# Loading the q weights of a decode kernel in two column halves, one issued by SyncE and one by ScalarE

## The chip, the cores and the metric

The kernel runs on one core of a Trainium2 chip. The metric is the device time of one execution, in microseconds (us); lower is better. Where two kernels are compared, both ran on the same chip in alternating rounds. Single executions of the same kernel fall on two close levels about 1 us apart (for the kernel before on one chip, 379.8 to 380.3 and 380.9 to 381.3), so a difference of half a microsecond between medians means little here.

## The reference

One decode step for 4 sequences: attention over the last 4096 positions of a cache, then a gated MLP, both with a residual.

```python
x: (4, 1, 576)   k_cache, v_cache: (4, 16, 16384, 128)   wq: (576, 4096)   wo: (4096, 576)
q = layernorm(x) @ wq                      # 32 query heads of 128
k, v = the last 4096 positions of the caches, each of the 16 heads used by 2 query heads
o = softmax(q k^T / sqrt(128)) v
h = x + o @ wo
gate, up = layernorm(h) @ W_gate, layernorm(h) @ W_up      # (576, 4608) each
h2 = h + (relu(gate) * up) @ W_down                        # (4608, 576)
```

All is bf16. With 4 tokens every weight and every cache entry is used for hardly any arithmetic: about 160 MB must be read from HBM for a few small products.

## The kernel before

A helper class `Prog` collects the instructions of each engine in program order and turns named dependencies into semaphore waits. `P.dma("sync", ...)` issues a load from SyncE, `P.dma("scalar", ...)` from ScalarE. Each engine works through its own list in order.

The loads go into an arena in SBUF with a ring of four 4 MB slots. Here is their order; all but the load of x are issued by SyncE (names shortened, cuts marked):

```python
NSLOT = 4; TILE = 16384; QWW = 8192        # columns of bf16 per partition

def place(name, off, size, reader, make, key=None):
    # waits for the last reader of every 64-column block it overwrites, then:
    P.dma("sync", ("L",) + name, make, semk, deps)

s = ring_slot()                            # wq: rows 0..511 as [128 partitions, 4 rows x 4096]
wq_off = slot0 + s * TILE
place(("wq", 0), wq_off, TILE, "QMM",
      lambda e: e.dma_start(out=arena[:, wq_off:wq_off + TILE], in_=main_rows(A_wq)), key=f"slot{s}")
P.dma("sync", ("L", "wq", 1), ...)         # the last 64 rows of wq, 0.5 MB
for g in range(NTILE):                     # 16 tiles of K and of V, 4.2 MB each
    add_kv("K", g)
    if g >= 4:
        add_kv("V", g - 4)
# ... the last V tiles, wo, W_gate, W_up, W_down
```

So the ring is filled in the order wq, K0, K1, K2, then K3 in the slot of wq, K4 in that of K0, V0 in that of K1, K5 in that of K2, V1 in that of K3, K6 in that of K4, and so on. A load into a used slot is issued only when the last reader is done: K3 after the q matmuls (`QMM`), K4 after the scores of tile 0.

The path from x to the first scores:

```python
act("warm_sqrt", ...)                                   # ScalarE's list before the change starts here
P.dma("scalar", ("L", "x"), lambda e: e.dma_start(out=x_bf, in_=A_x ...), "d_x")     # 4.5 KB
# VectorE: layer norm of x (bn_stats ... xn); PE: transposes; VectorE: xnT
for c in range(5):                                      # contraction chunks of 128 (the last of 64)
    for bk in range(2):
        for g in range(4):
            # chunk c < 4 reads columns c*4096.. of the wq slot, chunk 4 the 0.5 MB piece
            deps = {0: [("L", "wq", 0), "xnT", "c_xnT"], 4: [("L", "wq", 1)]}.get(c, [])   # at bk == g == 0
            pe(...)
# ScalarE and VectorE: q out of PSUM; PE: regroup; ScalarE: 8 copies of q into the score layout ("QW")
# VectorE: transpose each K tile in place (two halves, "TRA"); PE: scores, after "TRA" and for tile 0 after "QW"
```

VectorE transposes all 16 K tiles, and between the two halves of tile 4 it also does the softmax work of the first sequence.

Of the kernel before, what the change touches and what calls it, by code (L numbers as in the profile page):

```python
# [25 lines left out]
TILE = 16384  # L26
QWW = 8192
# [5 lines left out]
def mm_same(e, out, lhsT, rhs, start, stop, tile, pos):  # L33
    return e.add_instruction(mybir.InstMatmult(  # L34
        name=e.bass.get_next_instruction_name(), engine=mybir.EngineType.PE, ins=[e.lower_ap(rhs), e.lower_ap(lhsT)],
        outs=[e.lower_ap(out)], start_tensor_calc=start, stop_tensor_calc=stop, tile_size=tile, tile_position=pos,
        ldweights=False, bass_skip_group_check=True))
# [85 lines left out]
def bass_sequential_preLN__sliding_block_cached__glu_gated_reglu__decode_kernel(  # L123
# [12 lines left out]
    with ExitStack() as es:  # L136
        cnt = [0]

        def sb(name, shape, dt):
            return es.enter_context(nc.sbuf_tensor("sb_" + name, shape, dt))  # L140

        P = Prog()
# [8 lines left out]
        arena = sb("arena", [128, AW], BF16)  # L151
# [26 lines left out]
        xnT = sb("xnT", [128, DC + 1, 32], BF16)  # L178
# [36 lines left out]
        owner = {}  # L215
# [3 lines left out]
        def place(name, off, size, reader, make, key=None):  # L219
            deps = []  # L220
            for blk in range(off // 64, (off + size) // 64):
                r = owner.get(blk)
                if r is not None and r not in deps:
                    deps.append(r)
                owner[blk] = reader
            semk = key or "d_" + "_".join(str(v) for v in name)
            P.dma("sync", ("L",) + name, make, semk, deps)
            land[name] = off
# [3 lines left out]
        def ring_slot():  # L232
            s = ring[0] % NSLOT
            ring[0] += 1
            return s
# [12 lines left out]
        def main_rows(W):  # L248
            return W[0:512, :].rearrange("(p r) n -> p (r n)", r=4)

        def last_rows(W):
            return W[512:576, :].rearrange("r (a n) -> (r a) n", a=2)

        s = ring_slot()
        wq_off = slot0 + s * TILE
        place(("wq", 0), wq_off, TILE, "QMM",
              lambda e: e.dma_start(out=arena[:, wq_off:wq_off + TILE], in_=main_rows(A_wq)), key=f"slot{s}")
        P.dma("sync", ("L", "wq", 1), lambda e: e.dma_start(out=pT[:, 0:2048], in_=last_rows(A_wq)), "d_wq1")
        for g in range(NTILE):
            add_kv("K", g)  # L260
# [22 lines left out]
        for j in range(4):  # L283
            wd_off.append(off)
            for r0, r1 in ((0, 9),) if j < 3 else ((0, 6), (6, 8), (8, 9)):
                place(("wd", j, r0), off + r0 * D, (r1 - r0) * D, ("DOWN", 1),
                      lambda e, off=off, j=j, r0=r0, r1=r1: e.dma_start(  # L287
                          out=arena[:, off + r0 * D:off + r1 * D],
                          in_=B_W_down[j * 1152:(j + 1) * 1152, :].rearrange("(p r) n -> p (r n)", p=128)[:, r0 * D:r1 * D]))
# [18 lines left out]
                                                in_=c_qm[:, :, :].rearrange("p q (h j) -> p q h j", j=4),  # L308
# [4 lines left out]
                                                in_=to_v[:, :, :].rearrange("p n (k a) -> p n k a", a=4),  # L313
# [60 lines left out]
        def pe_q():  # L374
            for c in range(DC):
                for bk in range(2):
                    for g in range(4):
                        n = 4 * bk + g
                        w = arena[:, wq_off + c * H * DH + n * 512:][:, 0:512] if c < 4 else pT[:, g * 512:g * 512 + 512]
                        deps = []  # L380
                        if bk == g == 0:
                            deps = {0: [("L", "wq", 0), "xnT", "c_xnT"], 4: [("L", "wq", 1)]}.get(c, [])
                        if c < 4 and bk:
                            fn = lambda e, c=c, w=w, g=g, bk=bk: mm_same(e, bank[4 + bk][32 * g:32 * g + 32, :], xnT[:, c, :], w,
                                                                         c == 0, False, (128, 32), (0, 32 * g))
                        else:
                            fn = lambda e, c=c, w=w, g=g, bk=bk: e.matmul(  # L387
                                bank[4 + bk][32 * g:32 * g + 32, :], lhsT=xnT[:, c + bk if c == 4 else c, :], rhs=w,
                                start=(c == 0), stop=(c == 4), skip_group_check=True)
                        pe("QMM" if bk else "QMM0", fn, deps)  # L390
            for blk in range(8):
                pe("QT", lambda e, blk=blk: e.matmul(
                    bass.AP(tensor=psb, offset=7 * 512 + blk // 4 * 16 + blk % 4, ap=[[4096, 128], [4, 4], [32, 4]]),
                    lhsT=bass.AP(tensor=pp, offset=4096 + blk * 128, ap=[[PPW, 128], [1, 128]]),
                    rhs=bass.AP(tensor=ident_b, offset=0, ap=[[128, 128], [32, 4], [1, 4]]),
                    start=True, stop=True, skip_group_check=True), [f"qev{blk // 4}"] if blk % 4 == 0 else [])
# [166 lines left out]
        pe_x()  # L563
        dve_x()
        pe_q()
        act_q()
        dve_q()
# [49 lines left out]
        for a in range(8):  # L617
            for n in range(2):
                for j in range(4):
# [4 lines left out]
                    else:  # L624
# [6 lines left out]
                                             in_=bass.AP(tensor=psb, offset=512 + 224, ap=[[4096, 128], [1, 64], [0, 2]])), ["part1"])  # L631
# [28 lines left out]
        for g in range(2):  # L660
            for c in (4, 0, 1, 2, 3):
                part_ = c if c == 4 or (c == 3 and g) else 0
                for m in range(3):
                    for j in range(4):
                        first = m == 0 and j == 0 and (c in (0, 4) or part_ == 3)
                        deps = [("L", "gu", g, part_)] if first else []
# [36 lines left out]
        for j in range(4):  # L703
            wv = arena[:, wd_off[j]:wd_off[j] + WDJ].rearrange("p (r n) -> p r n", n=D)
            for r in range(9):
                for n in range(2):
                    deps = []
# [11 lines left out]
        for n in range(2):  # L719
            P.dma(("sync", "scalar")[n], ("O", n), lambda e, n=n: e.dma_start(  # L720
                out=orow[:, 288 * n:288 * n + 288], in_=bass.AP(tensor=out_sb, offset=32 * n * 288, ap=[[8 * 288, 4], [1, 288]])),
# [31 lines left out]
```

## Time and profile before

| | before |
|---|---|
| median time | 380.82 us (3 runs, 380.12 to 381.21; a fourth was taken with the change, below) |
| span of the profiled run | 378.4 us (that run took 380.22 us) |
| moved | 159.76 MB, mean 422 GB/s |
| PE, VectorE busy | 56%, 61% of the span |

These are the lines of the page of before that show what limits it. The row of digits gives the mean busy share of the 16 DMA engines in 40 slices of the span, in tenths (9 is 90% or more); the row below it gives what they moved.

```profile
span 378.4 us, 2668 instructions
...
DMA  8999999999999999999999999999999999999994
GB/s 333 443 441 429 414 433 440 443 426 416 435 434 443 423 421 436 436 440 419 423 436 436 436 423 429 435 436 433 423 429 438 429 436 423 441 421 422 416 426 190
...
q1 hardware_dynamic: 6632, 159.59, 98.4%
...
DMA 61%; PE 19%; DVE 15%; issue 4%; SPq 1%
```

The DMA engines are busy for 90% or more of every slice between the first and the last. No compute engine comes near that. The chain of waits that ended last (the final line) is mostly DMA. In the first slice only 333 GB/s were moved: 3.15 MB in 9.46 us, which at 436 GB/s (what many of the full slices moved) is 7.2 us of work, so by this estimate the start costs about 2.2 us.

The next lines are from the timeline of before: start, duration, engine, line, operation and, in brackets, the idle time before it and what ended it. SPq and ACTq are the issues of loads by SyncE and ScalarE.

```profile
0.73 0.38 SPq L257 DMA_DIRECT2D sb_arena<-in_A_wq_dram  x1
...
0.90 0.56 ACTq L343 DMA_DIRECT2D sb_x_bf<-in_A_x_dram  x1
...
5.67 0.81 DVE L345 BATCH_NORM_STATS2 sb_bn<-sb_x_bf 4x6 f32<-4x288 bf16 x2 [2.68 <-DMA sb_x_bf<-in_A_x_dram]
...
12.98 0.62 PE L387 MATMUL psb<-sb_arena,sb_xnT 128*32 128x512 bf16 x4 [4.23 <-DMA sb_arena<-in_A_wq_dram]
...
16.37 0.98 PE L387 MATMUL psb<-sb_pp,sb_xnT 128*32 128x512 bf16 x8
...
20.80 9.69 ACT L422 COPY sb_arena<-sb_q_keep 32x256 bf16<-32x256 bf16 x8
...
23.96 8.77 DVE L431 STREAM_TRANSPOSE sb_arena<-sb_arena 128x4096 f32<-128x4096 f32 x2 [2.38 <-DMA sb_arena<-in_A_k_cache_dram]
...
32.79 0.66 PE L455 MATMUL psb<-sb_arena 128*32 128x512 bf16 x4 [12.63 <-DVE sb_arena L431]
...
34.09 8.77 DVE L431 STREAM_TRANSPOSE sb_arena<-sb_arena 128x4096 f32<-128x4096 f32 x2 [1.36 <-DMA sb_arena<-in_A_k_cache_dram]
...
43.80 8.78 DVE L431 STREAM_TRANSPOSE sb_arena<-sb_arena 128x4096 f32<-128x4096 f32 x2 [0.94 <-DMA sb_arena<-in_A_k_cache_dram]
...
85.14 0.54 SPq L245 DMA_DIRECT2D sb_arena<-in_A_k_cache_dram  x1
...
374.06 1.36 PE L713 MATMUL psb<-sb_arena,sb_pp 128*32 128x288 bf16 x18 [0.77 <-DMA sb_arena<-in_B_W_down_dram]
```

The reader is to see three things. The first q matmul waits for wq, not for x, which was there 7 us earlier. VectorE waits for each of the first K tiles, so it keeps pace with the loads. And the last matmuls wait for the last piece of W_down. (The issue at 85.14 us is that of K6.)

### The profile page before, as it was taken

What the parts mean: (1) busy time and instruction counts of PE and PEld (TensorE: products, weight loads), DVE (VectorE), ACT (ScalarE), POOL (GpSimd) and SP (SyncE); (2) the same over time, 40 slices, a digit from 0 to 9 for tenths busy, and PEclk for the clock granted to TensorE, in tenths of its full rate; (3) what the DMA queues carried; (4) which work ended last, traced back from release to release, by engine and by line L of the source; (5) the groups of instructions that cost most, each with busy time, mean ns of one, the idle gap of its engine ahead of it and who ended that gap; (6) DMA issues with size and microseconds to landing.
All of it is one profiled execution on the core that took longest, in us unless ns stands there. A gap on an engine that the chain in (4) does not pass through costs nothing.

```text
span 378.4 us, 2668 instructions
## 1 busy us (share of the span) xinstructions
PE 213.3 (56%) x1471; PEld 38.3 (10%) x703; DVE 230.6 (61%) x206; ACT 54.2 (14%) x89; POOL 21.9 (6%) x44
## 2 busy tenths in 40 slices
PE   0404443149919191739291935674746598876774
PEld 0000000001101010101010100010101010003322
DVE  3178989779392959593838777766568523343220
ACT  3192000301000113010101130101010500122010
POOL 8860000000000000000000000000000000000000
PEclk9955888759958697687788895968796988998689
DMA  8999999999999999999999999999999999999994
GB/s 333 443 441 429 414 433 440 443 426 416 435 434 443 423 421 436 436 440 419 423 436 436 436 423 429 435 436 433 423 429 438 429 436 423 441 421 422 416 426 190
DMA packets 6660, 159.76 MB, mean 422 GB/s; under 512 B 748, under 2 KB 888, under 8 KB 1528
## 3 DMA queue, kind: packets, MB, share of 16 engines
q1 hardware_dynamic: 6632, 159.59, 98.4%
q8 instruction: 8, 0.13, 0.1%
q14 instruction: 4, 0.03, 0.0%
q10 hardware_dynamic: 16, 0.01, 0.0%
HBM read 159.58 MB, written 0.00 MB: 422 GB/s over the span
## 4 chain that ended last, share of the span: by engine, by line
DMA 61%; PE 19%; DVE 15%; issue 4%; SPq 1%
DMA sb_arena<-in_A_k_cache_dram 52%; DVE sb_arena L431 13%; PE psb L34 11%; DMA sb_arena<-in_B_W_down_dram 9%; PE psb L455 4%; PE psb L519 3%; DVE sb_o_tmp L532 1%; DVE sb_pp L497 1%; PE psb L545 0%; PE psb L713 0%; SPq L245 0%; PE psb L486 0%; SPq L287 0%; DVE sb_fq L543 0%; DVE sb_out_sb L716 0%
## 5 line engine op out<-in xcount | busy, mean ns | idle before, releaser
L431 DVE STREAM_TRANSPOSE sb_arena<-sb_arena 128x4096 f32<-128x4096 f32 x32 | 140.7, 4429 | 63.8 <-DMA sb_arena<-in_A_k_cache_dram 63.8
L34 PE MATMUL psb<-sb_arena,sb_pp 128*128 128x512 bf16 x384 | 106.6, 387 | 0.0
L455 PE MATMUL psb<-sb_arena 128*32 128x512 bf16 x256 | 44.3, 639 | 107.3 <-DVE sb_arena L431 107.3
L519 PE MATMUL psb<-sb_arena,sb_pp 128*128 128x512 bf16 x128 | 50.2, 392 | 9.3 <-DVE sb_o_tmp L532 9.3
L34 PE MATMUL psb<-sb_arena 128*32 128x512 bf16 x256 | 45.1, 643 | 0.0
L529 ACT COPY sb_o_tmp<-psb 32x512 f32<-32x512 f32 x32 | 18.5, 577 | 182.8 <-PE psb L34 182.5
L532 DVE TENSOR_TENSOR sb_o_tmp<-psb,sb_fm 32x512 f32<-32x512 f32 x32 | 21.7, 678 | 18.6 <-PE psb L34 18.1
L455 PEld LDWEIGHTS psb<-sb_arena 128*32 128x32 bf16 x256 | 9.7, 118 | 150.0 <-DVE sb_arena L431 120.2
L519 PEld LDWEIGHTS psb<-sb_arena,sb_pp 128*128 128x128 bf16 x128 | 12.7, 99 | 115.0 <-issue 115.0
L536 DVE TENSOR_REDUCE sb_o_sel<-sb_o_tmp 128x128 f32<-128x512 f32 x16 | 17.7, 1104 | 0.5
L476 ACT ACTIVATE sb_pp<-psb,sb_stat 128x512 bf16<-128x512 f32 x8 | 5.4, 682 | 80.9 <-DVE sb_stat L471 80.9
L497 DVE TENSOR_SCALAR sb_pp<-psb,sb_m 128x512 bf16<-128x512 f32 x16 | 10.8, 738 | 4.6 <-PE psb L486 4.6
L329 POOL TENSOR_SCALAR_AFFINE_SELECT sb_toq<-sb_toq 128x128 f32<-128x128 f32 x16 | 12.6, 788 | 2.3
L500 ACT ACTIVATE sb_pp<-psb,sb_m 128x512 bf16<-128x512 f32 x16 | 9.8, 697 | 12.7 <-PE psb L486 12.7
L535 DVE TENSOR_TENSOR sb_o_tmp<-sb_o_tmp,sb_fm 64x512 f32<-64x512 f32 x16 | 11.0, 690 | 0.5
L422 ACT COPY sb_arena<-sb_q_keep 32x256 bf16<-32x256 bf16 x8 | 9.7, 1445 | 0.1
L545 PE MATMUL psb<-sb_fq,sb_toq 128*128 128x4 f32 x8 | 1.8, 301 | 12.2 <-DVE sb_fq L543 12.2
L486 PE MATMUL psb<-sb_pp,sb_to_v 128*32 128x256 bf16 x64 | 4.3, 403 | 6.0 <-DVE sb_pp L480 6.0
L480 DVE STREAM_TRANSPOSE sb_pp<-sb_pp 128x512 bf16<-128x512 bf16 x8 | 5.5, 712 | 3.4 <-ACT sb_pp L476 3.4
L408 DVE CAST sb_pp<-psb 128x512 bf16<-128x512 f32 x1 | 2.4, 2425 | 8.1 <-PE psb L387 8.1
L713 PE MATMUL psb<-sb_arena,sb_pp 128*32 128x288 bf16 x72 | 5.9, 319 | 2.6 <-DMA sb_arena<-in_B_W_down_dram 2.6
L684 DVE TENSOR_TENSOR sb_pp<-psb,sb_pp 128x384 bf16<-128x384 f32 x3 | 1.5, 551 | 8.4 <-PE psb L675 8.4
(126 smaller groups left out, 91.6 us busy)
## 6 DMA issues: line engine op xcount, KB each, us to landing
sb_arena<-in_A_k_cache_dram SPq DMA_DIRECT2D x16, 4096.0 KB, 26.0
sb_arena<-in_A_v_cache_dram SPq DMA_DIRECT2D x16, 4096.0 KB, 27.9
sb_arena<-in_A_wo_dram SPq DMA_DIRECT2D x1, 4608.0 KB, 26.3
sb_arena<-in_B_W_gate_dram SPq DMA_DIRECT2D x1, 4608.0 KB, 27.8
sb_arena<-in_A_wq_dram SPq DMA_DIRECT2D x1, 4096.0 KB, 12.2
sb_arena<-in_B_W_down_dram SPq DMA_DIRECT2D x3, 1296.0 KB, 31.9
sb_arena<-in_B_W_up_dram SPq DMA_DIRECT2D x1, 3456.0 KB, 28.8
sb_arena<-in_B_W_up_dram SPq DMA_DIRECT2D x1, 1152.0 KB, 31.2
```

Source lines behind the costliest of these rows:

```text
L34: return e.add_instruction(mybir.InstMatmult(name=e.bass.get_next_instruction_name(), engine=mybir.EngineType.PE, ins=[e.lower_ap(rhs), e. ...
L329: pool(f"c_toq{q + 1}", lambda e, q=q: e.affine_select(out=toq[:, :, :, :], in_=toq[:, :, :, :], pattern=[[0, 16], [-32, 4], [-1, 2]], com ...
L422: act("QW", lambda e, i=i, q=q: e.copy(out=bass.AP(tensor=arena, offset=32 * i * AW + 2 * i + q, ap=[[AW, 32], [512, 16], [136, 4], [32, 4]]),
L431: dve(("TRA", g, w), lambda e: e.transpose(out=dst, in_=src), [("L", "K", g)] if w == 0 else [])
L455: fn = lambda e, out_=out_, lhsT=lhsT, rhs=rhs, start=start, stop=stop: e.matmul(out_, lhsT=lhsT, rhs=rhs, start=start, stop=stop, skip_gr ...
L497: dve(("EV", b, 1), lambda e, out_=out_, src=src, a=a: e.tensor_scalar(out=out_, in0=src, scalar1=m4[:, a:a + 1], scalar2=None, op0=ALU.mu ...
L500: act(("EV", b, 0), lambda e, out_=out_, src=src, a=a: e.activation(out=out_, in_=src, func=ACT.Copy, scale=m4[:, a:a + 1]), deps + (["c_m ...
L519: fn = lambda e, lhsT=lhsT, rhs=rhs, k=k, j=j: e.matmul(bank[2 + j], lhsT=lhsT, rhs=rhs, start=(k == 0), stop=(k == 7), skip_group_check=True)
L529: act(("OSC", g), lambda e, j=j: e.copy(out=o_tmp[32 * j:32 * j + 32, 0:512], in_=bank[2 + j][32 * j:32 * j + 32, :]), [("PV", g), ("OSEL" ...
L532: dve(("OSD", g), lambda e, j=j: e.tensor_tensor(out=ot(32 * j, 32), in0=bank[2 + j][32 * j:32 * j + 32, :].rearrange("p (t d) -> p t d", ...
L535: dve(("OS", g), lambda e: e.tensor_tensor(out=ot(64, 64), in0=ot(64, 64), in1=fmb(64, 64), op=ALU.mult), [("OSC", g)])
L536: dve(("OSEL", g), lambda e: e.tensor_reduce(out=o_sel[:, qd, b, :], in_=o_tmp[:, 0:512].rearrange("p (t d) -> p d t", d=DH), axis=AX.X, o ...
```

## The change

The intent is to start the two halves of wq at the same time from two engines, so that the q weights come in sooner or their issue costs less. The 4 MB piece becomes two of 2 MB: chunks 0 and 1 from SyncE, chunks 2 and 3 from ScalarE.

```diff
-        place(("wq", 0), wq_off, TILE, "QMM",
-              lambda e: e.dma_start(out=arena[:, wq_off:wq_off + TILE], in_=main_rows(A_wq)), key=f"slot{s}")
+        place(("wq", 0), wq_off, QWW, "QMM",
+              lambda e: e.dma_start(out=arena[:, wq_off:wq_off + QWW], in_=main_rows(A_wq)[:, 0:QWW]), key=f"slot{s}")
+        for blk in range((wq_off + QWW) // 64, (wq_off + TILE) // 64):
+            owner[blk] = "QMM"
+        P.dma("scalar", ("L", "wq", 2), lambda e: e.dma_start(out=arena[:, wq_off + QWW:wq_off + TILE], in_=main_rows(A_wq)[:, QWW:2 * QWW]),
+              "d_wq2")
...
-                            deps = {0: [("L", "wq", 0), "xnT", "c_xnT"], 4: [("L", "wq", 1)]}.get(c, [])
+                            deps = {0: [("L", "wq", 0), "xnT", "c_xnT"], 2: [("L", "wq", 2)], 4: [("L", "wq", 1)]}.get(c, [])
```

What the diff does not say aloud: the new issue stands in ScalarE's list ahead of the load of x.

## The prediction

> **What bounds the kernel now: the loads.** The page counts 159.6 MB in a span of 378.4 us. Between 46 and 340 us the stretch table gives a DMA share of 1.00 at 432 GB/s, against 0.60 for PE and 0.66 for DVE. The chain of waits: 61% DMA. The time is about 2.2 us of start (3.15 MB moved in the first 9.5 us is 7.2 us of work at 436 GB/s), some 370 us of streaming and 4.4 us of tail after the last W_down piece at 374.0 us. The Trainium skill ("DMA: Bandwidth & Descriptors", Where 436 GB/s comes from) puts the ceiling at 435 GB/s; this trace is at it.
>
> **What the change does.** The 4 MB load of wq (issued at 0.73 us, landing 12.2 us later) becomes two of 2 MB, one on ScalarE's queue. Bytes and later loads stay. It adds one issue (0.38 us on SyncE, 0.56 for x on ScalarE). The same page (Issuing engines are not separate DMA queues) says that such issues interleave on the same 16 engines and save only sequencer time. The issue of wq was over by 1.1 us and the engines are full from about 2.2, so there is nothing to win. Both halves should land near 12 to 13 us.
>
> **The side effect expected.** ScalarE now issues its half before the tiny x load, on the same queue. x landed at about 5.6 us; layer norm and transposes ran from 5.67 (BATCH_NORM_STATS) to 9.2 us. Now x queues behind 2 MB moving at half rate and should land near 12.5 to 13.5 us. xnT is then ready near 16 to 17, and the q matmuls (12.98 to 17.35 before) run at about 16.5 to 21 us: q is 3 to 4.5 us later, not earlier. ScalarE's q copies (20.8 to 30.5 us) end near 34, so the first score matmuls start near 34.5 instead of 32.8.
>
> **How much is critical: nothing.** A late q can delay only the issue of loads. K3 takes wq's slot and is issued after the q matmuls (17.4 us, would become 21), but its turn comes when K2 has landed, 43.8 us. K4 is issued after the scores of tile 0 (36.8, would become 38.5) and is needed by about 53. Every K and V load takes at least 17.9 us from issue to landing where its own 4.2 MB take 9.7, so 8 us of work or more lie ahead of each. DVE waits for K1 until 34.09 and K2 until 43.80 us, so it is back in step by the second or third tile.
>
> **Predicted time: 380.8 us, 8 in 10 between 379.5 and 382.1.** Faster by over 2%: 0.01; within 2%: 0.97; slower by over 2%: 0.02.
>
> **What would show each step.** The second queue carries about 2.1 MB; total and mean rate stay (422 GB/s). BATCH_NORM_STATS starts near 13 us; the first q matmul waits for x's vector chain, not for wq; the q matmuls end near 21. The transposes of K1 and K2 start within 0.5 us of 34.1 and 43.8. The last W_down piece lands within 1 us of 374.0.
>
> **What would make it wrong.** Two queues at once might lower the rate (16 KB rows in place of 32 KB): a microsecond or two. If x lands behind the K tiles too, q could slip past the 16 us of slack and starve the queue. A gain would need an engine start-up that two queues shorten.

## The result, and the profile after

After the change the median is 380.55 us (4 runs, 380.13 to 381.04), against 380.54 us before (4 runs, the three above and one more, 380.12 to 381.21). The ratio is 0.9999, with a 95% interval from 0.9976 to 1.0022. Here and below a ratio is the mean time of one kernel's fast runs over that of the other's of the same rounds, so it is not quite the ratio of the medians quoted.

The page of after, the lines that answer to those above:

```profile
span 378.3 us, 2669 instructions
...
DMA  8999999999999999999999999999999999999994
GB/s 329 447 441 423 417 437 437 440 419 423 442 430 440 419 424 443 430 437 416 437 429 440 437 416 440 428 437 433 423 433 431 433 433 426 432 425 419 424 426 197
...
q1 hardware_dynamic: 6632, 157.49, 97.1%
q10 hardware_dynamic: 160, 2.10, 1.3%
...
DMA 61%; PE 18%; DVE 15%; issue 4%; SPq 1%
```

2.10 MB moved from SyncE's queue q1 to ScalarE's q10, and the total and its course are the same. The first slice moved 329 GB/s where it was 333: two queues did not start the engines sooner.

The timeline of after (line numbers are 4 higher from the changed lines on):

```profile
0.74 0.38 SPq L257 DMA_DIRECT2D sb_arena<-in_A_wq_dram  x1
0.75 0.42 ACTq L260 DMA_DIRECT2D sb_arena<-in_A_wq_dram  x1
...
1.27 0.53 ACTq L347 DMA_DIRECT2D sb_x_bf<-in_A_x_dram  x1
...
13.18 0.81 DVE L349 BATCH_NORM_STATS2 sb_bn<-sb_x_bf 4x6 f32<-4x288 bf16 x2 [10.18 <-DMA sb_x_bf<-in_A_x_dram]
...
17.06 0.62 PE L391 MATMUL psb<-sb_arena,sb_xnT 128*32 128x512 bf16 x4 [0.56 <-issue]
...
20.43 0.72 PE L391 MATMUL psb<-sb_pp,sb_xnT 128*32 128x512 bf16 x8
...
24.60 9.74 ACT L426 COPY sb_arena<-sb_q_keep 32x256 bf16<-32x256 bf16 x8
...
34.48 0.62 PE L459 MATMUL psb<-sb_arena 128*32 128x512 bf16 x4 [10.53 <-ACT sb_arena L426]
...
43.70 8.77 DVE L435 STREAM_TRANSPOSE sb_arena<-sb_arena 128x4096 f32<-128x4096 f32 x2 [0.96 <-DMA sb_arena<-in_A_k_cache_dram]
...
85.65 0.54 SPq L245 DMA_DIRECT2D sb_arena<-in_A_k_cache_dram  x1
...
374.02 1.36 PE L717 MATMUL psb<-sb_arena,sb_pp 128*32 128x288 bf16 x18 [0.77 <-DMA sb_arena<-in_B_W_down_dram]
```

The issues of the two halves do overlap (0.74 and 0.75 us), but x, 4.5 KB, now comes in at 13.18 us instead of 5.67. The trace names nothing that released the first q matmul ("<-issue"), but both halves of wq had landed by 13.3 us and VectorE was writing xnT until 16.96 us, so it is x that it waited for. It starts at 17.06 instead of 12.98 us, and the q matmuls end at 21.15 (20.43 + 0.72) instead of 17.35 us. q is 3.8 us later. The first scores wait for ScalarE's copies of q (over at 34.34 us) and not for VectorE, and start 1.7 us later. At K2 VectorE waits for the load again, as before (43.70 and 43.80 us), and the last piece of W_down is used at 374.02 against 374.06 us. A delay of 3.8 us at the front has vanished.

That leaves two readings. Either q never was on the path that sets the time (the theory of the prediction), or the split won some microseconds at the start and the late x gave the same back (the rival: two effects that cancel). The total alone can't tell them apart.

### The profile page after: what moved, and what is told of

It is laid out like the page before. It is cut to its first block, busy times and chain, and to the rows that moved or that the text cites. A ratio compares the mean times of both kernels' runs of the same rounds, so it can differ in the third digit from the quotient of the medians.

```text
span 378.3 us, 2669 instructions
## 1 busy us (share of the span) xinstructions
PE 212.5 (56%) x1471; PEld 37.8 (10%) x703; DVE 230.6 (61%) x206; ACT 54.3 (14%) x89; POOL 21.8 (6%) x44
## 4 chain that ended last, share of the span: by engine, by line
DMA 61%; PE 18%; DVE 15%; issue 4%; SPq 1%
DMA sb_arena<-in_A_k_cache_dram 52%; DVE sb_arena L435 13%; PE psb L34 11%; DMA sb_arena<-in_B_W_down_dram 9%; PE psb L459 4%; PE psb L523 3%; DVE sb_o_tmp L536 1%; DVE sb_pp L501 1%; PE psb L549 0%; PE psb L717 0%; SPq L245 0%; PE psb L490 0%; SPq L291 0%; DVE sb_fq L547 0%; DVE sb_out_sb L720 0%
## 5 line engine op out<-in xcount | busy, mean ns | idle before, releaser
L459 PE MATMUL psb<-sb_arena 128*32 128x512 bf16 x256 | 42.1, 630 | 104.0 <-DVE sb_arena L435 93.5
L34 PE MATMUL psb<-sb_arena 128*32 128x512 bf16 x256 | 43.5, 646 | 0.0
L540 DVE TENSOR_REDUCE sb_o_sel<-sb_o_tmp 128x128 f32<-128x512 f32 x16 | 17.7, 1107 | 0.5
L504 ACT ACTIVATE sb_pp<-psb,sb_m 128x512 bf16<-128x512 f32 x16 | 9.7, 692 | 12.8 <-PE psb L490 12.8
L349 DVE BATCH_NORM_STATS2 sb_bn<-sb_x_bf 4x6 f32<-4x288 bf16 x2 | 0.8, 440 | 10.2 <-DMA sb_x_bf<-in_A_x_dram 10.2
## 6 DMA issues: line engine op xcount, KB each, us to landing
sb_arena<-in_A_wq_dram SPq DMA_DIRECT2D x1, 2048.0 KB, 12.3
sb_arena<-in_A_wq_dram ACTq DMA_DIRECT2D x1, 2048.0 KB, 12.5
```

What stands on the lines that cost most here:

```text
L34: return e.add_instruction(mybir.InstMatmult(name=e.bass.get_next_instruction_name(), engine=mybir.EngineType.PE, ins=[e.lower_ap(rhs), e. ...
L459: fn = lambda e, out_=out_, lhsT=lhsT, rhs=rhs, start=start, stop=stop: e.matmul(out_, lhsT=lhsT, rhs=rhs, start=start, stop=stop, skip_gr ...
L504: act(("EV", b, 0), lambda e, out_=out_, src=src, a=a: e.activation(out=out_, in_=src, func=ACT.Copy, scale=m4[:, a:a + 1]), deps + (["c_m ...
L540: dve(("OSEL", g), lambda e: e.tensor_reduce(out=o_sel[:, qd, b, :], in_=o_tmp[:, 0:512].rearrange("p (t d) -> p d t", d=DH), axis=AX.X, o ...
```

## The experiments

"q ends" is the start plus the length of the last group of q matmuls in the timeline of the one profiled run of each kernel. e1, e2, e4 and e5 ran on one chip, e6 and the three e3 runs on another, e7 on a third.

| run | q ends, us | median, us | before, us | ratio (95%) |
|---|---|---|---|---|
| e5: halves in turn on SyncE | 15.7 | 379.97 | 380.01 | 0.9995 (0.9982 to 1.0007) |
| e1: the change, x first | 16.4 | 379.91 | 380.01 | 0.9994 (0.9981 to 1.0007) |
| (before) | 17.35 | | | |
| e2: wq whole, x behind it | 20.7 | 379.98 | 380.01 | 0.9996 (0.9982 to 1.0009) |
| (the change) | 21.15 | 380.55 | 380.54 | 0.9999 (0.9976 to 1.0022) |
| e7: x inside K0 | 27.9 | 380.80 | 380.11 | 1.0011 (0.9995 to 1.0027) |
| e3: x behind K0 | 32.2 | 383.20 | 380.12 | 1.0074 (1.0051 to 1.0098) |
| e3: x behind K1 | 41.1 | 392.94 | 380.12 | 1.0327 (1.0302 to 1.0352) |
| e3: x behind K2 | 51.6 | 402.55 | 380.12 | 1.0584 (1.0563 to 1.0605) |
| e4: two queues to K2 | 17.9 | 380.29 | 380.01 | 1.0008 (0.9995 to 1.0022) |
| e6: second half not loaded | 12.9 | 375.20 | 380.12 | 0.9872 (0.9846 to 0.9898) |

### e1: the split without the late x

The change, with the load of x moved ahead of ScalarE's half of wq. If two effects cancel, this leaves the gain alone.

```diff
+        P.dma("scalar", ("L", "x"), lambda e: e.dma_start(out=x_bf[:, :], in_=A_x.rearrange("b s d -> (b s) d")), "d_x")
         P.dma("scalar", ("L", "wq", 2), ...
...
-        P.dma("scalar", ("L", "x"), ...)
```

> The change with x issued ahead of ScalarE's half of wq. Theory (loads set the time, q has slack): x lands by 6 us, the first q matmul waits for wq and starts near 13 us as before, not at 17.06; the time is that of before within 0.3% (379.7 to 381.5). Rival (cancelling: the split wins time at the start and the late x gives the same back): with x early the win is left alone, so 2 to 4 us faster (about 377.5).

Measured: 379.91 us, ratio 0.9994; the 2 to 4 us of the rival lie far outside the interval, which leaves room for a gain of 0.7 us at most. The detail of the expectation was off: q did not start near 13 us. From the timeline of e1:

```profile
10.58 0.62 PE L391 MATMUL psb<-sb_arena,sb_xnT 128*32 128x512 bf16 x4 [3.03 <-DMA sb_arena<-in_A_wq_dram]
...
13.65 0.62 PE L391 MATMUL psb<-sb_arena,sb_xnT 128*32 128x512 bf16 x4 [1.17 <-DMA sb_arena<-in_A_wq_dram]
```

SyncE's half arrived first, so chunks 0 and 1 began at 10.58 us, and chunks 2 and 3 waited until 13.65 us for ScalarE's. The two queues did not share the engines evenly: the list of issues gives 9.8 us to landing for SyncE's half (issued at 0.74 us) and 12.3 us for ScalarE's (issued at 1.35 us, behind x). They landed 3.1 us apart, far more than the 0.6 us between their issues. q ended 0.95 us earlier than before, and the time did not move.

### e2: the late x without the split

wq whole as before; only x goes to SyncE's queue, behind the 4 MB of wq.

```diff
+        P.dma("sync", ("L", "x"), lambda e: e.dma_start(out=x_bf[:, :], in_=A_x.rearrange("b s d -> (b s) d")), "d_x")
         P.dma("sync", ("L", "wq", 1), ...
...
-        P.dma("scalar", ("L", "x"), ...)
```

> Before, wq whole, only x issued behind the 4 MB of wq on SyncE's queue. Theory: x lands near 13 us, the q matmuls run at about 17 to 21.3 us as after the change, and the time is that of before within 0.3%. Rival (cancelling): the late x is left alone without the split's win, so 2 to 4 us slower (about 384).

Measured: 379.98 us, ratio 0.9996. VectorE's layer norm began at 12.93 us and q ended at 20.7 us, nearly as late as with the change, and it cost nothing. With e1 this settles the rival: neither half of the supposed cancellation shows. The intervals leave at most 0.7 us for the gain (e1) and 0.3 us for the loss (e2). It also shows that the late x comes from its place behind a large load, whichever engine issues it.

### e5: the earliest q

Both halves of wq on SyncE, one after the other; x alone on ScalarE as before. This should give what the change was after, an earlier start of the q matmuls.

```diff
-        P.dma("scalar", ("L", "wq", 2), ...
+        P.dma("sync", ("L", "wq", 2), ...
```

> Both halves of wq on SyncE one after the other, x as before on ScalarE. Here the first half should land near 7.5 us, so the q matmuls start when x is ready, at about 9.3 us, and stop for the second half, which lands near 12.5: q ends near 15.2 us instead of 17.35, about 2 us earlier. Theory: this gives nothing, the time stays within 0.3% of before. Rival (the q chain is on the critical path): about 2 us faster.

Measured: 379.97 us, ratio 0.9995. The timeline of e5:

```profile
8.48 0.62 PE L391 MATMUL psb<-sb_arena,sb_xnT 128*32 128x512 bf16 x4 [0.56 <-DMA sb_arena<-in_A_wq_dram]
...
12.95 0.62 PE L391 MATMUL psb<-sb_arena,sb_xnT 128*32 128x512 bf16 x4 [2.57 <-DMA sb_arena<-in_A_wq_dram]
...
32.74 0.62 PE L459 MATMUL psb<-sb_arena 128*32 128x512 bf16 x4 [14.21 <-DVE sb_arena L435]
```

In turn on one queue the first half is usable by 8.48 us, 4.5 us before the whole was; side by side on two queues in the changed kernel both halves landed near 13 us. So for an early start one queue is the better tool. But q ends only 1.65 us earlier (15.7 us), and the first scores still start at 32.74 us, because they wait for VectorE, which waits for K0 to land.

### e4: do two queues move bytes faster?

e1, and K0, K1 and K2 in column halves on the two queues as well.

```diff
+            if kind == "K" and g < 3:
+                place((kind, g), off, TILE, ("QK", g),
+                      lambda e: e.dma_start(out=arena[:, off:off + QWW], in_=src[:, :, 0:QWW]), key=f"slot{s}")
+                P.dma("scalar", ("L", "Kb", g),
+                      lambda e: e.dma_start(out=arena[:, off + QWW:off + TILE], in_=src[:, :, QWW:2 * QWW]), f"d_kb{g}")
+                return
...
-            dve(("TRA", g, w), ..., [("L", "K", g)] if w == 0 else [])
+            dve(("TRA", g, w), ..., [("L", "K", g)] + ([("L", "Kb", g)] if g < 3 else []) if w == 0 else [])
```

> e1, and K tiles 0 to 2 also in two column halves on the two queues: about 8.4 MB on each queue. Theory: the 16 engines are full with one queue, so the rate stays: K tile 1 lands at about 34.1 us and K tile 2 at about 43.8 as before (within 0.5), and the time within 0.3%. Rival (two queues lift the rate or the start): K tile 2 lands 1 us or more before 43.8 and the time falls by as much; or, if switching costs, it lands 1 us or more later.

Measured: 380.29 us, ratio 1.0008 with an interval that includes 1. In the table of stretches for e4 (stretch and its length, busy time and count of each engine, granted clock, DMA share, GB/s):

```profile
2.00:10.00 8.00, 0.47 (x10) 0.39 (x10) 3.34 (x14) 3.16 (x5) 7.28 (x17) 1.00 0.93 389
10.00:20.00 10.00, 4.84 (x40) 0.69 (x25) 2.06 (x1) 2.44 (x1) 8.42 (x12) 1.00 1.01 431
20.00:30.00 10.00, 0.58 (x8) 0.37 (x8) 5.43 (x11) 9.12 (x10) 5.04 (x9) 1.00 1.01 428
30.00:44.00 14.00, 3.86 (x32) 0.52 (x16) 12.65 (x4) 1.05 (x1) 0.00 (x0) 0.97 1.00 427
```

and for before:

```profile
2.00:10.00 8.00, 0.47 (x10) 0.39 (x10) 3.23 (x14) 2.00 (x5) 7.28 (x17) 1.00 0.96 406
10.00:20.00 10.00, 4.75 (x48) 1.19 (x32) 2.42 (x1) 2.43 (x1) 8.42 (x12) 1.00 0.99 426
20.00:30.00 10.00, 0.15 (x4) 0.05 (x2) 7.41 (x11) 9.68 (x10) 5.07 (x9) 0.53 0.98 420
30.00:44.00 14.00, 5.05 (x44) 0.76 (x24) 11.70 (x4) 0.49 (x1) 0.00 (x0) 0.62 1.03 445
```

Length times rate adds up to 17.7 MB for e4 and 17.9 MB for before between 2 and 44 us: two queues moved no more. The first two K tiles came later than expected, since both halves of a tile must be there and the queues drifted apart (transposes of K0 at 26.61 instead of 23.96 us, of K1 at 36.74 instead of 34.09 us). K2, the last of the split tiles, was in time: its later half, SyncE's, landed 41.1 us after its issue, where the whole of K2 took 40.8 us before. So the bytes of the three tiles took as long as with one queue, and only their order differed. The interval includes no change, but the four runs on the lower level (380.21 to 380.47) all lie above the eight of before on that level (379.89 to 380.16). A loss of about 0.3 us is therefore likely; what causes it is not shown.

### e6: fewer bytes

Its output is wrong, which doesn't matter for the time. The second half of wq is not loaded, and chunks 2 and 3 use the first half again. All compute stays. The edit is shown against the changed kernel; the wait for the second half goes too.

```diff
-        P.dma("scalar", ("L", "wq", 2), ...)
...
-                        w = arena[:, wq_off + c * H * DH + n * 512:]...
+                        w = arena[:, wq_off + c % 2 * H * DH + n * 512:]...
```

> Wrong result on purpose: the second half of wq (2.1 MB) is not loaded, the matmuls of chunks 2 and 3 use the first half again; x alone on ScalarE. All compute stays. Theory (bytes set the time): 2.1 MB at 432 GB/s are 4.85 us, so about 375.7 us, every K tile landing about 4.8 us earlier. Rival (compute or q sets the time, bytes at the start are hidden): within 1 us of before.

Measured: 375.20 us against 380.12, so 4.9 us less for 2.10 MB; at 432 GB/s they take 4.85 us. The last matmuls of W_down start at 368.89 us instead of 374.06:

```profile
368.89 1.37 PE L715 MATMUL psb<-sb_arena,sb_pp 128*32 128x288 bf16 x18 [0.77 <-DMA sb_arena<-in_B_W_down_dram]
```

Bytes at the front of the queue count in full at the end. (q ends 4.4 us earlier in this run as well. e5 has shown only that 1.65 us of that alone give nothing, but here too VectorE waits for the load of K0, until 19.23 us, so it is again the loads that pass on the gain.)

### e3: how late may q be?

Before, with x on SyncE's queue behind K0, K1 or K2. The theory claims slack, so it must also say where the slack ends.

```diff
             add_kv("K", g)
+            if g == 0:        # 1 and 2 in the other two
+                P.dma("sync", ("L", "x"), ...)
...
-        P.dma("scalar", ("L", "x"), ...)
```

> Before with x issued on SyncE's queue behind wq and K tile 0. x should land near 24 us, xnT be ready near 28, q end near 32.3 (15 us later than before); K3 is then issued near 32.3, ahead of its turn at 43.8, and K4 near 50, ahead of its turn at about 53.5. Theory (slack of 16 to 26 us before a load is issued too late): time within 1 us of before. Rival (no slack, q's delay is passed on): about 15 us slower.

Measured: 383.20 us, 3.1 us slower. This was a miss: neither "within 1 us" nor the rival's 15. The hole is not at K3 or K4, where the prediction had looked, but at K6. The timeline of this run has

```profile
36.29 39.07 DVE L432 STREAM_TRANSPOSE sb_arena<-sb_arena 128x4096 f32<-128x4096 f32 x9
...
92.22 0.54 SPq L245 DMA_DIRECT2D sb_arena<-in_A_k_cache_dram  x1
```

and its table of stretches (the last number is GB/s)

```profile
88.00:90.00 2.00, 1.73 (x16) 0.46 (x12) 2.00 (x2) 0.00 (x0) 0.00 (x0) 0.50 0.91 393
90.00:92.00 2.00, 2.00 (x20) 0.18 (x4) 2.00 (x1) 0.00 (x0) 0.00 (x0) 0.95 0.69 295
92.00:94.00 2.00, 2.00 (x13) 0.29 (x3) 2.00 (x2) 0.00 (x0) 0.00 (x0) 1.00 0.53 147
94.00:96.00 2.00, 2.00 (x11) 0.20 (x2) 2.00 (x1) 0.00 (x0) 0.00 (x0) 1.00 0.96 393
```

VectorE starts the transposes of K0 12.3 us late (36.29 instead of 23.96 us) and then runs nine of them without a pause, so it is catching up, but slowly: a tile takes it 8.77 us, and the loads bring one in about 9.7. Then comes the softmax work between the halves of tile 4. The scores of tile 4, which free the slot of K6, are still late, and K6 is issued at 92.22 us instead of 85.14, 7.1 us late. By then the queue has run dry: finer stretches of the trace show hardly any bytes between 91.6 and 93.4 us. In the page's 40 slices the slice with this hole moved 305 GB/s where a full one moves about 430, which is 2.8 us of its 9.56 us. Of 7.1 us of lateness about 4 were free, and 3.1 were paid.

> The same with x behind K tile 1. x near 34.5 us, q ends near 42.8, K3 issued at about 42.8, about 1 us ahead of its turn, with some 1.5 us from issue to first bytes: about 1 us of idle engines. The scores of tile 0 end near 60, K4 is issued at about 60 where its turn is near 54.5: about 6 to 8 us idle. Theory: about 7 to 9 us slower (388 to 390), with a gap in the DMA share before K4. Rival (no slack): 25 us slower.

Measured: 392.94 us, 12.8 us slower, 3 to 5 more than expected. The hole before K4 is there (0 to 16 GB/s between 52 and 58 us, and 131 until 60), and a second one before K6 that the expectation lacked (0 GB/s between 100 and 102 us, K6 issued at 101.19 us). K3, issued at 41.15 us, was in time.

> The same with x behind K tile 2. x near 44.2 us, q ends near 52.5: K3 issued about 8.7 us after the queue ran dry at 43.8, about 10 us idle; K4 issued near 70 where its turn is near 64: 6 to 8 us idle more. Theory: 16 to 19 us slower (397 to 400). Rival (no slack): 35 us slower.

Measured: 402.55 us, 22.4 us slower, again 3 to 6 more than expected, for the same reason: beside the holes before K3 (issued at 51.64 us, the engines at 4 GB/s or less from 42 to 52.5) and before K4 (0 from 64 to 70) there is one from 110 to 112 us (16 GB/s), before K6 (issued at 111.62 us).

### e7: the revised slack

x between two column halves of K0, so that q is about 10 us late. The transposes of K0 wait for both halves, and the load of x on ScalarE goes.

```diff
+            if kind == "K" and g == 0:
+                P.dma("sync", ("L", "Ka", g), lambda e: e.dma_start(out=arena[:, off:off + QWW], in_=src[:, :, 0:QWW]), "d_ka")
+                P.dma("sync", ("L", "x"), ...)
+                place((kind, g), off, TILE, ("QK", g),
+                      lambda e: e.dma_start(out=arena[:, off + QWW:off + TILE], in_=src[:, :, QWW:2 * QWW]), key=f"slot{s}")
+                return
```

> Before with K tile 0 loaded in two column halves on SyncE's queue and x issued between them: x should land near 18.5 us, q end near 26.5, about 9 us later than before (15 later cost 3.1 us in the run with x behind K tile 0). Revised theory: the load that runs late first is K6, whose slot is freed by the scores of tile 4, and about 4 us of its lateness are free. DVE starts K tile 0 about 7 us late here (12.3 in the run with x behind K tile 0) and makes up about 5 of it by tile 4, so K6 is issued about 2 us late, near 87, and nothing is lost: time within 0.3% of before. Rival (any q delay costs in proportion, 3.1 us for 15): 1.8 us slower, 381.9.

Measured: ratio 1.0011, interval 0.9995 to 1.0027. The rival's 1.8 us (a ratio of 1.0047) is outside; a loss of up to 1 us can't be excluded. The median, 380.80 us, lies 0.7 us above that of before, but the six runs are two at 379.9 and four between 380.8 and 381.2, the two levels that the kernel before shows as well. In the profiled run (379.91 us) K6 was issued at 87.85 us, 2.7 us late, and its stretches show no hole:

```profile
87.85 0.54 SPq L251 DMA_DIRECT2D sb_arena<-in_A_k_cache_dram  x1
...
88.00:90.00 2.00, 2.00 (x11) 0.20 (x2) 2.00 (x2) 0.00 (x0) 0.00 (x0) 1.00 0.91 393
90.00:92.00 2.00, 2.00 (x11) 0.29 (x3) 2.00 (x1) 0.00 (x0) 0.00 (x0) 1.00 0.92 393
92.00:94.00 2.00, 2.00 (x11) 0.20 (x2) 0.88 (x3) 0.00 (x0) 0.00 (x0) 1.00 1.14 492
```

So the dose table has a knee. Up to q ending 10.6 us late nothing clear is lost. At 14.8 us late 3.1 us are lost, which puts the knee at about 11.7 us (an estimate: 14.8 minus 3.1, if every microsecond beyond it is paid). Beyond it about every microsecond is paid: the time rises by 9.7 us for the 8.9 us from 32.2 to 41.1, and by 9.6 us for the 10.5 us from 41.1 to 51.6. No run lies between 10.6 and 14.8 us. The change uses 3.8 us, well short of the knee wherever it lies between them.

No version tried beats both kernels: e1 and e5 lie within 0.1 us of before in the median, inside their intervals.

## Why the prediction was right

- **What bounds the kernel.** Right, and now shown in both directions: 2.1 MB fewer save 4.9 us (e6), and q 1.65 us earlier saves nothing that the runs resolve (e5).
- **Nothing to win in issue or bandwidth.** Right. 380.55 us against 380.8 predicted, the last W_down piece within 0.04 us of before. e4 shows no gain even with 8.4 MB on ScalarE's queue.
- **The late x.** Right in each step: layer norm at 13.18 us ("12.5 to 13.5" for x), xnT copied by about 17 us, q matmuls from 17.06 to 21.15 us ("16.5 to 21"), q's copies over at 34.34 us ("near 34"), first scores at 34.48 us ("near 34.5"). e2 reproduces it without the split.
- **Back in step.** Right: at K2 VectorE waits for the load again.
- **The size of the slack.** The prediction named K3 and K4 and warned of "the 16 us of slack", and it counted "8 us of work or more" ahead of each load, from the 17.9 us between issue and landing less 9.7 for the load itself. The conclusion held, but this term was too large. The load with 17.9 us is K6. Issue to landing also contains the delay before the first bytes (1.2 us for K6 in e3 with x behind K0: issued at 92.22 us, bytes from 93.4 us) and that after the last (1.2 us or more in e3 with x behind K2, where the bytes of K2 stop at 42.0 us, a few KB more, by their size x, follow until 42.6 us, and VectorE gets x at 43.78 us). Taking both from the 8.2 us leaves, by estimate, about 5 to 6 us, and about 4 us of K6's lateness proved free (e3 with x behind K0). Because VectorE catches up by only about a microsecond a tile, K6 and not K4 is the first to be late, and q has about 11.7 us (the knee estimated above), not 16. The forecast of the total did not hang on this: the change needed 3.8 us.
- **Both halves near 12 to 13 us.** Right for the changed kernel (12.3 and 12.5 us after issue, so at 13.0 and 13.3 us). In e1, with x first on ScalarE's queue, they landed 3.1 us apart, so even sharing is not to be relied on. Why the shares differ stays open.

## What to carry to other kernels

Where the DMA engines are full from start to end, as here, expect a second issuing engine only to change the order in which the same bytes arrive; look at what it pushes back, above all a tiny load that now stands behind a large one in the same queue. Before calling a delay harmless, follow it to every later load whose buffer it frees, and compare the lateness of the issue with when the queue runs dry, not with issue-to-landing times. To show that something is off the critical path, move it by known amounts in both directions until the time does change: the knee is the slack.

## What the Trainium skill lacked or had wrong

- "DMA: Bandwidth & Descriptors", Issuing engines are not separate DMA queues: its statement that loads from several engines interleave on the same 16 engines and save only sequencer time agrees with the rates here (between 10 and 44 us 427 to 431 GB/s with two queues in e4, 420 to 445 with one); no run tested the saving of sequencer time. It lacks the warning that follows for small loads: 4.5 KB issued at 1.27 us behind 2 MB on the same queue was usable at 13.18 us; at 5.67 us when issued at 0.90 us on ScalarE's queue with the 4 MB ahead on the other; and by 2.91 us in e1, issued at 0.75 us ahead of ScalarE's half.
- The same page, Queues, rings and completion order, says that each DMA engine goes round its queues packet by packet. It gives no figure for the shares: halves of equal size landed 12.3 and 12.5 us after issue in the changed kernel, but 9.8 and 12.3 us in e1, where the second was issued 0.6 us after the first.
- The same page, Where 436 GB/s comes from: 435 GB/s as the ceiling agrees with the 432 GB/s of this trace between 46 and 340 us (a short stretch can read higher: 445 GB/s between 30 and 44 us, at a DMA share of 1.03). Its advice that the HBM side, at about 358 GB/s, binds for loads from HBM does not fit this single core, which held 432 GB/s on such loads. That passage lacks the proviso of "Perfetto Trace Analysis", Roofline, which gives 358 GB/s as the share of a core when both cores of a pair read, and about 435 GB/s as the bound of one alone.
